# A gated mix of recurrent memory attention and a GLU, one core: one Wo piece kept in spare PSUM columns, one buffer for H

## The chip, the cores and the metric

The kernel runs on one core of a Trainium2 chip. The metric is the device time of one execution in microseconds (us); lower is better. Engines are named as in the profile: PE (matrix), PEld (its weight loads), DVE (vector), ACT (scalar), POOL, SP (it issues DMAs here). ACT issues DMAs too, on a queue of its own. SBUF is the working memory, PSUM the eight banks that PE writes.

## What is computed

x is 2048 rows of 640 (bf16). Two parts are mixed by a gate of each row. The costly part, `a`, runs over 64 segments of 32 rows, each with 8 memory rows that come from the segment before, so that the segments follow one another strictly:

```python
for s in range(n_seg):                                  # 64 segments, seg_len 32
    h = jnp.concatenate([mem, xs], axis=1)              # 8 memory rows + 32 rows of x
    q, k, v = (einsum('btd,dhe->bhte', h, W) for W in (Wq, Wk, Wv))   # 640 -> 32 heads x 192
    scores = einsum('bhqe,bhke->bhqk', q, k) * 192 ** -0.5            # causal, memory visible to all
    p = softmax(where(mask, scores, -1e9))
    o = einsum('bhqk,bhke->bhqe', p, v)
    o = einsum('bhte,hed->btd', o, Wo)
    mem = o[:, :8]                                      # goes on to the next segment
    outs.append(o[:, 8:])
b = (gelu(x @ w_gate) * (x @ w_up)) @ w_down
out = g * a + (1 - g) * b,   g = sigmoid((x * gate_w).sum(-1))
```

## The kernel before

**Stages.** The feed-forward part `b` comes first and goes to a scratch tensor in HBM. Then a left phase computes Q and K of the rows of x that become "left" columns of each segment (the last 8 of 32), for all segments at once, and stores them to scratch. Then the loop over 64 segments runs, about 27 us each by the profile.

**A segment** treats the 32 heads in four octets of eight. The list `PROG` gives the order in which a segment's work is recorded: for an octet `q` and `k` (`cmode`: 20 matmuls of 128x384 over five pieces of the weight, then an evacuation on ACT into a row buffer, `rows_sb`), `tq`, `tk` (`row_transp`: DVE transposes the rows into `Qs` and `Ks`), `v` (`v_oct`), `sc` (`scores`: a mask matmul, 16 score matmuls, then maximum and subtraction on DVE), `ex` (`softmax`: exponential on ACT, the rest on DVE), `pt` (`p_transp`), `pv` (`pv_oct`: PV matmuls, evacuated by one ACT copy and by two DVE copies, "uT lo" and "uT hi"), and `wo` (`wo_part`: 10 matmuls for each of 24 pieces of Wo, each piece a pair of 128-row chunks, accumulated in bank 7). In segments with s%4 == 0 `v_oct` also computes V of the left columns (20 more matmuls an octet), and the output of the four segments before goes out through five transposes and a store. At a segment's end ACT copies the new memory rows from bank 7 into H of the next segment (L1059, "mem evac"), and then its first matmul may start. Octets go through PSUM banks 0 to 4 in turn (`misc_bank`); the scores use 5 and 6. A bank is guarded as a whole: who writes it waits for all who read it.

**The order.** Each engine runs its instructions in the recorded order. A small recorder (`S_.add` with the regions read and written) derives the semaphore waits; a PE operation with several waits hands some of them to the last matmuls of the operation before. Nothing reorders at run time.

**The weights.** Wq, Wk, Wv and Wo together, 245760 B a partition, do not fit SBUF. A planner at build time makes pieces of 3072 B a partition (384 KB; Q, K, V) and 2560 B (320 KB; Wo), 84 of them; 61 stay in SBUF (`res_off`, loaded once by SP, some of them late, during segment 0) and 23 are streamed in every segment through a ring of five slots on SP's queue (`issue_ring`, L551; a slot is loaded again once PE has read it). The planner raises the number of streamed pieces until the rest fits `res_cap`, and spreads them evenly over a cost estimate of the segment (`COST`, `tcons`). The 23 are 14 of Q, K, V and 9 of Wo.

**Buffers that the change touches.** `Hb`, two buffers of 320 B a partition, holds H transposed (the five 128-row blocks of the segment's 32 columns); `x_load(s + 1)` fills the next one by a DMA on ACT's queue behind `k` of octet 2. `Ks` (1280 B a partition) is followed in memory by the two row buffers (`rows`, 1536 B). Two blocks of `Ks` stay zero from the start (memsets on POOL, L826 and L827). `left_fill(s, o)` (POOL, L834 and L838) copies the left columns of an octet from the staging buffer into `Qs` and `Ks`; that of octet 0 of the next segment is recorded behind the scores of octet 3, with `stg_load`, the DMA that fills the staging buffer. A Q, K or V group uses columns 0 to 383 of its bank (as 4-byte words), a PV group at most 320, so that the last 128 words of banks 0 to 4 are unused in the loop.

## Time and profile before

| | |
|---|---|
| median of 3 runs | 2105.77 us (2099.25 to 2106.26) |
| the profiled execution | 2103.78 us; span 2102.0 us |
| mean granted PE clock | 0.987 |
| busy over the span | PE 86%, PEld 55%, DVE 58%, ACT 29%, POOL 12% |
| moved by DMA | 622.11 MB, mean 296 GB/s; of it 576.63 MB on SP's queue |
| SP's weight loads | Wo 591, Wk 404, Wq 276, Wv 272; 4.8 to 5.3 us from issue to landing |

Each row of the profile's groups names a source line, an engine, an operation, its output and inputs (`arena` is all of SBUF, `ps` all of PSUM), shapes, and a count; then total busy time in us, the mean of one in ns, and the idle time of the engine ahead of them with what ended it. A row of a window begins with its start and end in us and its length. In a row of waits stand the total in us, how often, and the longest. "PE <- DMA" idle time is told both for the matmuls (PE) and for the weight loads that run ahead of them (PEld); the ends of matmuls are modelled, so a matmul that waits in mid-group can look busy.

### The profile page before, as it was taken

What the parts mean: (1) busy time and instruction counts of PE and PEld (TensorE: products, weight loads), DVE (VectorE), ACT (ScalarE), POOL (GpSimd) and SP (SyncE); (2) the same over time, 40 slices, a digit from 0 to 9 for tenths busy, and PEclk for the clock granted to TensorE, in tenths of its full rate; (3) what the DMA queues carried; (4) which work ended last, traced back from release to release, by engine and by line L of the source; (5) the groups of instructions that cost most, each with busy time, mean ns of one, the idle gap of its engine ahead of it and who ended that gap; (6) DMA issues with size and microseconds to landing.
All of it is one profiled execution on the core that took longest, in us unless ns stands there. A gap on an engine that the chain in (4) does not pass through costs nothing.

```text
span 2102.0 us, 92054 instructions
## 1 busy us (share of the span) xinstructions
PE 1797.9 (86%) x40486; PEld 1147.2 (55%) x40486; DVE 1223.0 (58%) x3928; ACT 619.4 (29%) x1468; POOL 241.8 (12%) x1060
## 2 busy tenths in 40 slices
PE   7899966888888888888889888888888888888887
PEld 3454433565555555555556555656555555555555
DVE  2222324666666666666666665666666666666666
ACT  2222212333333323332333332332323333323232
POOL 0000001111111111111111111111111111111111
PEclk9999998999999999999999999999999999999999
DMA  9412569999999999999999999999999999999998
GB/s 369 148 35 71 150 186 299 326 320 336 312 327 321 321 310 318 319 321 320 316 323 331 324 325 316 310 330 318 325 322 327 329 326 321 324 320 327 310 329 276
DMA packets 374252, 622.11 MB, mean 296 GB/s; under 512 B 81490, under 2 KB 250714, under 8 KB 373850
## 3 DMA queue, kind: packets, MB, share of 16 engines
q1 hardware_dynamic: 302842, 576.63, 80.9%
q10 hardware_dynamic: 71008, 39.60, 6.6%
q8 instruction: 316, 5.18, 1.0%
q14 instruction: 86, 0.70, 0.1%
HBM read 595.01 MB, written 21.10 MB: 293 GB/s over the span
## 4 chain that ended last, share of the span: by engine, by line
DMA 39%; PE 36%; DVE 16%; ACTq 3%; ACT 3%; issue 2%; SPq 0%; DVEq 0%
DMA arena<-in_A_Wk_dram 16%; DMA arena<-in_A_Wo_dram 9%; DMA arena<-in_A_Wv_dram 8%; PE ps L1017 8%; PE ps L868 8%; PE ps L895 5%; DMA arena<-in_A_Wq_dram 5%; PE ps L803 4%; DVE arena L971 3%; PE ps L732 2%; PE ps L729 2%; ACTq L818 2%; DVE arena L1004 2%; PE ps L988 2%; DVE arena L1002 2%
## 5 line engine op out<-in xcount | busy, mean ns | idle before, releaser
L868 PE MATMUL ps<-arena 128*32 128x384 bf16 x10240 | 547.3, 329 | 95.2 <-DMA arena<-in_A_Wk_dram 32.4
L1017 PE MATMUL ps<-arena 128*128 128x40 bf16 x15360 | 457.3, 180 | 58.7 <-DVE arena L1004 38.6
L1017 PEld LDWEIGHTS ps<-arena 128*128 128x128 bf16 x15360 | 425.5, 96 | 103.3 <-DVE arena L1004 50.0
L868 PEld LDWEIGHTS ps<-arena 128*32 128x32 bf16 x10240 | 246.6, 96 | 307.2 <-DMA arena<-in_A_Wk_dram 83.8
L872 ACT ACTIVATE arena<-ps 128x384 bf16<-128x384 f32 x512 | 251.4, 491 | 524.3 <-PE ps L868 450.6
L895 PE MATMUL ps<-arena 128*32 128x384 bf16 x6400 | 327.5, 331 | 54.0 <-DMA arena<-in_A_Wv_dram 31.5
L834 POOL COPY arena<-arena 128x96 bf16<-128x96 bf16 x256 | 67.5, 264 | 1611.3 <-PE ps L927 1063.2
L895 PEld LDWEIGHTS ps<-arena 128*32 128x32 bf16 x6400 | 150.9, 97 | 184.4 <-DMA arena<-in_A_Wv_dram 73.0
L878 DVE STREAM_TRANSPOSE arena<-arena 128x384 bf16<-128x384 bf16 x256 | 146.0, 570 | 90.4 <-ACT arena L872 90.4
L971 DVE TENSOR_TENSOR arena<-ps,arena 128x320 bf16<-128x320 bf16 x256 | 125.9, 492 | 88.9 <-PE ps L969 83.4
L988 PE MATMUL ps<-arena 128*128 128x160 bf16 (+1 forms) x768 | 131.2, 261 | 52.1 <-DVE arena L974 51.1
L906 ACT ACTIVATE arena<-ps 128x384 bf16<-128x384 f32 x256 | 125.8, 491 | 164.6 <-PE ps L895 164.3
L998 ACT ACTIVATE arena<-ps 128x320 bf16<-128x320 f32 x256 | 110.7, 432 | 215.4 <-PE ps L990 215.4
L955 DVE TENSOR_REDUCE arena<-ps 104x4 f32<-104x160 f32 x256 | 82.9, 324 | 153.4 <-ACT ps L953 151.4
L838 POOL COPY arena<-arena 64x32 bf16<-64x32 bf16 (+1 forms) x768 | 165.9, 216 | 47.4
L885 DVE STREAM_TRANSPOSE arena<-arena 64x128 bf16<-64x128 bf16 x512 | 145.4, 284 | 8.1
L953 ACT ACTIVATE ps<-ps 104x160 f32<-104x160 f32 x256 | 73.9, 289 | 202.6 <-DVE ps L943 185.5
L990 PE MATMUL ps<-arena 128*128 128x64 bf16 (+1 forms) x768 | 124.9, 203 | 0.0
L988 PEld LDWEIGHTS ps<-arena 128*128 128x128 bf16 x768 | 72.7, 98 | 93.0 <-DVE arena L974 71.0
L941 DVE TENSOR_REDUCE arena<-ps 104x4 f32<-104x160 f32 x256 | 81.2, 317 | 71.7 <-PE ps L927 71.7
L881 DVE STREAM_TRANSPOSE arena<-arena 128x256 bf16<-128x256 bf16 x256 | 111.5, 436 | 12.6 <-ACT arena L872 12.6
L1002 DVE CAST arena<-ps 64x160 bf16<-64x160 f32 x256 | 80.2, 313 | 46.4 <-PE ps L990 42.4
(71 smaller groups left out, 1672.1 us busy)
## 6 DMA issues: line engine op xcount, KB each, us to landing
arena<-in_A_Wo_dram SPq DMA_DIRECT2D x591, 320.0 KB, 4.8
arena<-in_A_Wk_dram SPq DMA_DIRECT2D x404, 384.0 KB, 5.2
arena<-in_A_Wq_dram SPq DMA_DIRECT2D x276, 384.0 KB, 5.1
arena<-in_A_Wv_dram SPq DMA_DIRECT2D x272, 384.0 KB, 5.3
left_qk_scratch<-arena ACTq DMA_DIRECT2D x16, 768.0 KB, 7.9
arena<-left_qk_scratch ACTq DMA_DIRECT2D x64, 192.0 KB, 4.5
arena<-in_A_x_dram SPq DMA_DIRECT2D x4, 640.0 KB, 15.6
xt_scratch<-arena ACTq DMA_DIRECT2D x4, 640.0 KB, 9.0
```

Source lines behind the costliest of these rows:

```text
L838: S_.add("pool", lambda e, a=a, b=b, lo=lo, hi=hi, sa=sa: e.tensor_copy(out=Ks[lo:hi, a:b, L:R], in_=stg[lo:hi, o, 1, sa:sa + b - a]), rea ...
L868: S_.add("pe", [lambda e, j=j, k=k, gv=gv: e.matmul(ps[32 * j:32 * j + 32, bank, 0:384].rearrange("p (c i) -> p c i", i=32), Hb[hb][:, k, ...
L872: S_.add("act", lambda e: e.activation(out=rows_sb[m], in_=ps[:, bank, 0:384], func=ACTF.Copy), reads=[r_ps[bank]], writes=[r_rows[m]], na ...
L878: S_.add("dve", lambda e: e.transpose(out=Qs[:, :, 0:L], in_=rows_sb[0].rearrange("p (c r) -> p c r", r=L)), reads=[r_rows[0]], writes=[r_ ...
L885: S_.add("dve", lambda e, a=a, lo=lo: e.transpose(out=Ks[lo:lo + 64, a:a + 4, 0:L], in_=src[lo:lo + 64, :, 1]), reads=[r_rows[1]], writes= ...
L895: return [lambda e, j=j: e.matmul(ps[32 * j:32 * j + 32, bk, 0:384], lhs, g_[:, 384 * j:384 * (j + 1)], start=(k == 0), stop=(k == KT - 1) ...
L906: S_.add("act", lambda e: e.activation(out=v_sb[o % NVB], in_=ps[:, bank, 0:384], func=ACTF.Copy), reads=[r_ps[bank]], writes=[r_v[o % NVB ...
L971: S_.add("dve", lambda e: e.tensor_tensor(out=PTm, in0=apx(pv[:, 512:616], [[64, 2], [0, 4], [1, R]]), in1=apx(mbd, [[0, 2], [1, 4], [0, R]]),
L988: return [lambda e: e.matmul(full, v[:, e0:e0 + 128], PTm[:, ia:ib], start=True, stop=False, skip_group_check=True), lambda e: e.matmul(pa ...
L990: lambda e: e.matmul(part, vl[:, e0:e0 + 128], PTl[:, ia:ib], start=False, stop=True, skip_group_check=True)]
L1002: S_.add("dve", lambda e: e.tensor_copy(out=u[0:64, :, 1, :], in_=ps[0:64, B, 0:W].rearrange("p (t r) -> p t r", r=R)), reads=[r_ps[B]], w ...
L1017: fns.append(lambda e, g_=g_, i=i, c=c, n=n, tl=tl, cc=cc, u=u: e.matmul(ps[:, OB, n * R:(n + 1) * R], g_[:, i, n * 128:(n + 1) * 128], u[ ...
```

## The change

One piece of Wo, (3, 19), the second pair of the last Wo group, is neither resident nor streamed. Before the loop `held_init` loads it from HBM, transposes it on PE, copies it back to SBUF, and transposes it again into the last 256 bf16 columns of banks 0 to 4, so that it stands there as it was: 5 x 256 columns are its 1280. In each segment `held_copy` (L591 of the changed kernel) copies it on ACT, one copy for each bank, into the memory of `Ks` and of the row buffers, which are idle by then; it is recorded after the first two pairs of Wo group 1 (`("pw", 0)`). After the last Wo group POOL zeroes the two blocks of `Ks` again (`k_zero`), and only then `left_fill` for the next segment follows. H has one buffer; `x_load` for the next segment moves behind `v` of octet 3, the last reader of H. The planner, with 320 B more and 2560 B less to place, streams 22 pieces: 13 of Q, K, V and 9 of Wo, at other places of the list; the left phase loads 8 pieces through the ring instead of 10. The three memory layouts' other parts stay.

```diff
-    wsA["H"] = al(2 * KT * L * 2)
+    wsA["H"] = al(KT * L * 2)
...
-    Hb = [bview(o_H + b * KT * L * 2, KT * L * 2).rearrange("p (k r) -> p k r", r=L) for b in range(2)]
+    Hb = [bview(o_H, KT * L * 2).rearrange("p (k r) -> p k r", r=L)] * 2
...
-            ("wo", 0), ("pt", 2), ("sc", 3), ("ex", 3), ("pv", 2), ("wo", 1), ("wo", 2, 0), ("pt", 3), ("wo", 2, 1),
+            ("wo", 0), ("pt", 2), ("sc", 3), ("ex", 3), ("pv", 2), ("wo", 1, 0), ("pw", 0), ("wo", 1, 1), ("wo", 1, 2), ("wo", 2, 0), ("pt", 3), ("wo", 2, 1),
             ("pv", 3), ("wo", 2, 2), ("wo", 3)]
...
+    HELD = (3, 19)
+    held_i = order.index(HELD)
...
-            best = min((i for i in range(npieces) if i not in streamed), key=lambda i: abs(tcons[i] - target))
+            best = min((i for i in range(npieces) if i not in streamed and i != held_i), key=lambda i: abs(tcons[i] - target))
             streamed.add(best)
-        if tot_bytes - sum(piece_size(order[i]) for i in streamed) <= res_cap:
+        if tot_bytes - GO - sum(piece_size(order[i]) for i in streamed) <= res_cap:
             break
...
+        if key == HELD:
+            return piece_view(key, o_held), r_held
...
+    o_held = wsB_off["K"]
+    r_held = sreg(o_held, GO)
+
+    def held_copy(seg):
+        flat = bview(o_held, GO)
+        for b in range(5):
+            S_.add("act", lambda e, b=b: e.activation(out=flat[:, 256 * b:256 * b + 256], in_=psb(b)[:, 768:1024],
+                                                      func=ACTF.Copy),
+                   reads=[r_ps[b]], writes=[r_held], name="held s%d %d" % (seg, b))
...
+    def held_init():
+        t1, r1 = bview(wsB_off["Q"], GO), sreg(wsB_off["Q"], GO)
+        t2, r2 = bview(wsB_off["vl"], GO), sreg(wsB_off["vl"], GO)
+        S_.add("sp", lambda e: e.dma_start(t1.rearrange("p (c n) -> p c n", n=Dm), piece_src(HELD)), writes=[r1],
+               dma_sem="held", name="held load")
+        for b, c0, nb in ((5, 0, 8), (6, 8, 2)):
+            S_.add("pe", [... e.transpose(psb(b)[:, ...], t1[:, 128 * c:128 * (c + 1)], ident) ...], ..., name="heldT")
+            S_.add("dve", lambda e, b=b, c0=c0, nb=nb: e.tensor_copy(out=t2[:, ...], in_=psb(b)[:, 0:128 * nb]), ...)
+        for b in range(5):
+            S_.add("pe", [... e.transpose(psb(b)[:, 768 + 128 * i:896 + 128 * i], t2[:, ...], ident) for i in range(2)], ..., name="heldTT")
+
     issue_ring(0, B_RING - 1)
+    held_init()
     S_.add("pool", lambda e: e.memset(pl_sb, 0.0), writes=[r_p])
-    S_.add("pool", lambda e: e.memset(Ks[64:128, 8:12, :], 0.0), writes=[r_Kz[0]])
-    S_.add("pool", lambda e: e.memset(Ks[0:64, 12:16, :], 0.0), writes=[r_Kz[1]])
+
+    def k_zero():
+        S_.add("pool", lambda e: e.memset(Ks[64:128, 8:12, :], 0.0), writes=[r_Kz[0]])
+        S_.add("pool", lambda e: e.memset(Ks[0:64, 12:16, :], 0.0), writes=[r_Kz[1]])
+
+    k_zero()
...
         elif s + 1 < NSEG:
             stg_load(s + 1)
-            left_fill(s + 1, 0)
...
                 if kind == "k" and i == 2:
-                    if s + 1 < NSEG:
-                        x_load(s + 1)
...
             elif kind == "v":
                 v_oct(s, i)
+                if i == NOCT - 1 and s + 1 < NSEG:
+                    x_load(s + 1)
+            elif kind == "pw":
+                held_copy(s)
...
                 wo_part(s, item)
+        if s + 1 < NSEG:
+            k_zero()
+            left_fill(s + 1, 0)
```

How this moves instructions, at three places of a segment. First SP's queue, from octet 1 to the segment's last ring load; each row is a load through the ring, and "x9" are nine in a row. Before:

```order
L551 DMA arena<-in_A_Wq_dram 128x1536
L551 DMA arena<-in_A_Wk_dram 128x1536
L551 DMA arena<-in_A_Wv_dram 128x1536
L551 DMA arena<-in_A_Wq_dram 128x1536
L551 DMA arena<-in_A_Wk_dram 128x1536 x2
L551 DMA arena<-in_A_Wv_dram 128x1536
L551 DMA arena<-in_A_Wq_dram 128x1536
L551 DMA arena<-in_A_Wk_dram 128x1536 x2
L551 DMA arena<-in_A_Wv_dram 128x1536
L551 DMA arena<-in_A_Wo_dram 128x2x640 x9
```

and now:

```order
L553 DMA arena<-in_A_Wq_dram 128x1536
L553 DMA arena<-in_A_Wk_dram 128x1536
L553 DMA arena<-in_A_Wv_dram 128x1536
L553 DMA arena<-in_A_Wq_dram 128x1536
L553 DMA arena<-in_A_Wk_dram 128x1536
L553 DMA arena<-in_A_Wv_dram 128x1536 x2
L553 DMA arena<-in_A_Wq_dram 128x1536
L553 DMA arena<-in_A_Wk_dram 128x1536
L553 DMA arena<-in_A_Wv_dram 128x1536
L553 DMA arena<-in_A_Wo_dram 128x2x640 x9
```

One load of Wk is gone in octet 2, V of octet 2 takes two where K took two, and octet 3 has one of Wk instead of two; octet 1's three stay. The nine loads of Wo stay nine.

Second ACT, from the DMA of x for the next segment (`xt_scratch`) to the copy of the memory rows that ends the segment (128x5x8); 128x384 are the evacuations of Q, K and V, 104x160 the exponential, 128x2x4x40 the evacuation of PV. Before:

```order
L631 DMA arena<-xt_scratch 128x160
L953 ACTIVATE ps<-ps 104x160
L998 ACTIVATE arena<-ps 128x2x4x40
L906 ACTIVATE arena<-ps 128x384
L872 ACTIVATE arena<-ps 128x384 x2
L953 ACTIVATE ps<-ps 104x160
L998 ACTIVATE arena<-ps 128x2x4x40
L906 ACTIVATE arena<-ps 128x384
L830 DMA arena<-left_qk_scratch 128x768
L953 ACTIVATE ps<-ps 104x160
L998 ACTIVATE arena<-ps 128x2x4x40 x2
L1059 ACTIVATE arena<-ps 128x5x8
```

and now, from what was the fifth of these rows (the evacuations of Q and K of octet 3):

```order
L910 ACTIVATE arena<-ps 128x384 x2
L990 ACTIVATE ps<-ps 104x160
L1035 ACTIVATE arena<-ps 128x2x4x40
L944 ACTIVATE arena<-ps 128x384
L646 DMA arena<-xt_scratch 128x160
L868 DMA arena<-left_qk_scratch 128x768
L990 ACTIVATE ps<-ps 104x160
L1035 ACTIVATE arena<-ps 128x2x4x40
L591 ACTIVATE arena<-ps 128x256 x5
L1035 ACTIVATE arena<-ps 128x2x4x40
L1101 ACTIVATE arena<-ps 128x5x8
```

The load of x stands now behind the evacuation of V of octet 3, ahead of the staging load, and the five copies of the held piece between the last two evacuations of PV.

Third PE, with the waits, from the transposes of P of octet 3 (128x104) through two pairs of Wo (L1017, now L1054) to its PV matmuls (L988 and L990, now L1025 and L1027); e_dve and e_act are the semaphores of DVE and ACT, d_ring1 one of the ring's. Before:

```order
L968 MATMUL ps<-arena 128x104
L969 MATMUL ps<-arena 128x104
L1017 MATMUL ps<-arena 128x40 x10
L1017 MATMUL ps<-arena 128x40 [waits d_ring1]
L1017 MATMUL ps<-arena 128x40 x9
L988 MATMUL ps<-arena 128x160 [waits e_dve]
L990 MATMUL ps<-arena 128x4x16
L988 MATMUL ps<-arena 128x160
L990 MATMUL ps<-arena 128x4x16
L988 MATMUL ps<-arena 128x320
L990 MATMUL ps<-arena 128x8x16
```

and now:

```order
L1005 MATMUL ps<-arena 128x104
L1006 MATMUL ps<-arena 128x104
L1054 MATMUL ps<-arena 128x40 x10
L1054 MATMUL ps<-arena 128x40 [waits d_ring4]
L1054 MATMUL ps<-arena 128x40 x8
L1054 MATMUL ps<-arena 128x40 [waits e_dve]
L1025 MATMUL ps<-arena 128x160 [waits e_act]
L1027 MATMUL ps<-arena 128x4x16
L1025 MATMUL ps<-arena 128x160
L1027 MATMUL ps<-arena 128x4x16
L1025 MATMUL ps<-arena 128x320 [waits e_act]
L1027 MATMUL ps<-arena 128x8x16
```

PV of octet 3 waits now for ACT at its start and once more in its second half: for the copies out of banks 3 and 4. The wait for DVE, which it had before, has gone to the Wo matmul ahead of it.

More of the change, by code (lines that the diff above doesn't have):

```diff
@@ L351, in _build @@
     o_H = wsA_off["H"]
-    Hb = [bview(o_H + b * KT * L * 2, KT * L * 2).rearrange("p (k r) -> p k r", r=L) for b in range(2)]
-    r_Hm = [sreg(o_H + b * KT * L * 2, 8) for b in range(2)]
-    r_Hxp = [sreg(o_H + b * KT * L * 2 + 8, KT * L * 2 - 8) for b in range(2)]
+    Hb = [bview(o_H, KT * L * 2).rearrange("p (k r) -> p k r", r=L)] * 2
+    r_Hm = [sreg(o_H, 8)] * 2
+    r_Hxp = [sreg(o_H + 8, KT * L * 2 - 8)] * 2
     o_Hx = wsA_off["Hx"]
@@ L506, in _build @@
             target = (k + 0.5) * tseg / nstream
-            best = min((i for i in range(npieces) if i not in streamed), key=lambda i: abs(tcons[i] - target))
+            best = min((i for i in range(npieces) if i not in streamed and i != held_i), key=lambda i: abs(tcons[i] - target))
             streamed.add(best)
-        if tot_bytes - sum(piece_size(order[i]) for i in streamed) <= res_cap:
+        if tot_bytes - GO - sum(piece_size(order[i]) for i in streamed) <= res_cap:
             break
         nstream += 1
-    resident_list = [i for i in range(npieces) if i not in streamed]
+    resident_list = [i for i in range(npieces) if i not in streamed and i != held_i]
     stream_list = [i for i in range(npieces) if i in streamed]
@@ L578, in load_late @@
             late_done[0] += 1
+    o_held = wsB_off["K"]
+    assert wsB_off["K"] + al(16 * R * 2) == wsB_off["rows"]
+    r_held = sreg(o_held, GO)
[5 more added lines that the diff above has]
+                   reads=[r_ps[b]], writes=[r_held], name="held s%d %d" % (seg, b))
     left_stream = [order[i] for i in stream_list if order[i][0] < 2]
```

14 lines of the change are left out of this document (12 added, 2 removed).

## The prediction

> **What bounds the kernel now.** I read the 40 slices and the queues of the page first, then the 62 whole segments as one window, then the waits inside them.
>
> ```profile
> DMA  9412569999999999999999999999999999999998
> GB/s 369 148 35 71 150 186 299 326 320 336 312 327 321 321 310 318 319 321 320 316 323 331 324 325 316 310 330 318 325 322 327 329 326 321 324 320 327 310 329 276
> ...
> q1 hardware_dynamic: 302842, 576.63, 80.9%
> ...
> DMA 39%; PE 36%; DVE 16%; ACTq 3%; ACT 3%; issue 2%; SPq 0%; DVEq 0%
> ```
>
> From the seventh slice on, which is the loop over segments, the 16 DMA engines are busy nine tenths or more in every slice at a flat 310 to 336 GB/s. Nearly all of it is queue q1, SP's weight stream. The last row is the chain that ended last: DMA has its largest share, with PE close behind.
>
> ```profile
> L1059 ACT ACTIVATE arena<-ps x63: 204/204/204, 361.5 to 2069.3; 128x40 bf16<-128x40 f32 x63
> ...
> 361.69:2069.55 1707.86, 1467.48 (x37483) 979.80 (x37483) 1104.52 (x3671) 525.65 (x1303) 226.10 (x992) 1.00 0.96 322
> ```
>
> L1059 ends each segment once, so 62 segments last 2069.3 - 361.5 = 1707.8 us, 27.55 us each. The window over them gives length, then busy time of PE, PEld, DVE, ACT and POOL, granted clock 1.00, DMA share 0.96, 322 GB/s. 27.55 us at 322 GB/s are 8.87 MB a segment. The 23 streamed pieces (14 of 384 KB, 9 of 320 KB) are 8.45 MB of that.
>
> Is the DMA the limit, or only busy? The waits in that window, for SP, PEld and PE:
>
> ```profile
> SPq L551 <- PE ps L868: 207.5, 226, 3.7
> ...
> PEld ps L868 <- DMA arena<-in_A_Wk_dram: 78.4, 155, 2.1
> PEld ps L895 <- DMA arena<-in_A_Wv_dram: 70.6, 117, 2.0
> PEld ps L868 <- DMA arena<-in_A_Wq_dram: 58.6, 124, 2.5
> PEld ps L1017 <- DMA arena<-in_A_Wo_dram: 21.8, 44, 1.7
> ...
> PE ps L895 <- DMA arena<-in_A_Wv_dram: 30.9, 44, 1.6
> PE ps L868 <- DMA arena<-in_A_Wk_dram: 28.8, 52, 1.7
> PE ps L868 <- DMA arena<-in_A_Wq_dram: 21.8, 31, 2.1
> PE ps L1017 <- DMA arena<-in_A_Wo_dram: 16.1, 32, 1.6
> ```
>
> SP issues the next piece as soon as PE frees a slot, and PE in turn waits for landings: 97.6 us by its matmuls, 229.4 us by its weight loads, 1.57 and 3.70 us a segment. So the pieces arrive just as they are needed, in both halves of a segment:
>
> ```profile
> 1509.10:1520.60 11.50, 9.48 (x300) 8.13 (x298) 7.02 (x25) 2.80 (x8) 0.92 (x4) 1.00 1.00 330
> 1520.60:1536.10 15.50, 13.57 (x287) 7.24 (x288) 10.10 (x34) 5.51 (x13) 2.74 (x12) 1.00 0.98 353
> ```
>
> The first is a Wo half, where a chain over DVE (softmax, transposes, evacuations) paces PE; the second the Q/K/V half of the next segment. The DMA rests in neither: it fills the ring while PE follows DVE.
>
> A natural experiment is in the trace. Every fourth segment (s%4 == 0) has 80 more V matmuls and five transposes. The sums over 15 segments with s%4 == 0, and over 15 with s%4 == 1:
>
> ```profile
> sum 427.11, PE 386.11 PEld 264.27 DVE 300.90 ACT 127.64 POOL 54.68; mean PE 25.74 PEld 17.62 DVE 20.06 ACT 8.51 POOL 3.65
> ...
> sum 402.21, PE 341.81 PEld 226.29 DVE 256.56 ACT 127.22 POOL 54.70; mean PE 22.79 PEld 15.09 DVE 17.10 ACT 8.48 POOL 3.65
> ```
>
> PE has 2.95 us more to do and the segment gets 1.66 us longer (28.47 against 26.81). It also stores output, 160 KB or 0.51 us at 322 GB/s:
>
> ```profile
> out_dram<-arena ACTq DMA_DIRECT2D x16, 160.0 KB, 5.4
> ```
>
> That leaves 1.15 us for 2.95 us of PE work, 0.39 us per us: PE's work is largely, not wholly, hidden.
>
> **The change part by part.**
>
> *One transfer fewer.* The planner's budget gains 320 B a partition from H and leaves out the held 2560 B. 22 pieces are then streamed, 13 of 384 KB and 9 of 320 KB: 393216 B less a segment. At 322 GB/s that is 1.22 us, the upper price, if time follows bytes alone. For the lower price I split the time: without DMA waits a segment is about 27.55 - 3.70 = 23.85 us of PE and chain; at 0.39 us per us these carry 9.3 us of the 27.55, so 18.25, or 66%, go with the transfers: 0.66 x 1.22 = 0.81 us. The middle is 1.02. I take 1.02 for three segments of four, and 0.81 where s%4 == 0, since PE is already 25.74 of 28.47 us busy there: 48 x 1.02 + 16 x 0.81 = 62 us. All 64 at the ends: 52 and 78 us.
>
> *Five copies on ACT.* PSUM to SBUF, 128x256 bf16:
>
> ```profile
> L712 ACT ACTIVATE arena<-ps 128x1024 bf16<-128x1024 bf16 x4 | 4.1, 1024 | 9.8 <-PE ps L698 9.8
> ...
> 1510.50 0.49 ACT L906 ACTIVATE arena<-ps 128x384 bf16<-128x384 f32 x1 [0.35 <-PE ps L895]
> ...
> 1513.79 0.28 ACT L953 ACTIVATE ps<-ps 104x160 f32<-104x160 f32 x1 [2.80 <-DVE ps L943]
> ...
> 1514.11 0.33 DVE L955 TENSOR_REDUCE arena<-ps 104x4 f32<-104x160 f32 x1 [0.35 <-ACT ps L953]
> 1514.47 0.18 DVE L957 RECIPROCAL arena<-arena 104x4 f32<-104x4 f32 x1
> ...
> 1515.32 0.33 DVE L1004 CAST arena<-ps 64x160 bf16<-64x160 f32 x1
> ...
> 1517.26 0.24 PE L988 MATMUL ps<-arena 128*128 128x160 bf16 x1 [0.29 <-DVE arena L974]
> ...
> 1517.72 0.44 ACT L998 ACTIVATE arena<-ps 128x320 bf16<-128x320 f32 x1 [3.30 <-PE ps L990]
> ...
> 1520.38 0.20 ACT L1059 ACTIVATE arena<-ps 128x40 bf16<-128x40 f32 x1 [2.22 <-PE ps L1017]
> ```
>
> 40 columns take 204 ns (L1059) and 1024 take 1024, 0.833 ns a column, so 256 take 384 ns and five 1.92 us. ACT is idle 3.30 us ahead of L998 at 1517.72, and the copies stand right there. Their cost is not length but the banks: the last of them wait for L1004 of octet 2 (its bank is read by DVE), which ends at 1515.65, and PV of octet 3 at 1517.26 then waits for the copies of banks 3 and 4. Two copies after L1004, each with some 0.05 us for its wait on the one before (an estimate: L957 starts 0.03 us after L955, on which it waits), end at 1516.52; the third, which only PV's second half needs, at 1516.95. PV starts at 1517.26 for DVE's sake. Cost nothing, with 0.3 us in hand even for the third; if a copy took 0.49 us, as 384 columns do, the third would end at 1517.27. PE's wait on ACT is then one already over.
>
> *H in one buffer.* The x load goes from ACT's place behind k 2 to behind the V evacuation (L906 above, 1510.99); what needs it is L1059 at 1520.38.
>
> ```profile
> arena<-xt_scratch ACTq DMA_DIRECT2D x64, 40.0 KB, 5.3
> ```
>
> It lands at about 1516.3, with 4 us in hand. Behind it on ACT stand the stage load and the exponential of octet 3, which waits for DVE until 1513.79. Leaving k 2 it frees ACT ahead of the exponential of octet 1: a gain of at most 0.3 us, taken as nothing.
>
> *POOL.* Two memsets are added, and four copies that filled the next segment's K and Q columns early now wait for the held piece's matmuls.
>
> ```profile
> L834 POOL COPY arena<-arena 128x96 bf16<-128x96 bf16 x256 | 67.5, 264 | 1611.3 <-PE ps L927 1063.2 <-DMA arena<-left_qk_scratch 361.7 <-PE ps L1017 186.3
> L838 POOL COPY arena<-arena 64x32 bf16<-64x32 bf16 x512 | 105.2, 206 | 31.5
> L838 POOL COPY arena<-arena 128x64 bf16<-128x64 bf16 x256 | 60.6, 237 | 15.8
> L826 POOL MEMSET arena<- 64x160 bf16 x1 | 0.2, 226 | 0.1
> ...
> 359.67 1.72 PE L1017 MATMUL ps<-arena 128*128 128x40 bf16 x62 [0.32 <-DVE arena L1004]
> ...
> 365.90 0.25 PE L916 MATMUL ps<-arena 128*40 128x160 bf16 x2
> ```
>
> 2 x 226 + 264 + 237 + 2 x 206 = 1365 ns, some 1.7 us with gaps, from the end of the held piece (22 of the 62 matmuls, at 360.3) to 362.0. The first scores, which need them, start at 365.90. Cost nothing; 3.9 us of cover.
>
> *Start.* A load of 320 KB, 20 transposes and two copies stand ahead of segment 0 on PE.
>
> ```profile
> arena<-in_A_x_dram SPq DMA_DIRECT2D x4, 640.0 KB, 15.6
> ...
> 137.28 1.29 PE L698 MATMUL ps<-arena 128*128 128x128 bf16 x20
> ...
> 322.32 3.23 PE L895 MATMUL ps<-arena 128*32 128x384 bf16 x37 [21.61 <-DMA arena<-left_xt_scratch]
> ```
>
> PE idles 21.61 us there for another queue's load. Even 15.6 us for the held load, 1.3 of transposes and three 1.02 us steps for the copies fit. Cost nothing, at worst a few us once; two ring loads fewer in the left phase are left at nothing too.
>
> Sum: 62 us. The profiled execution took 2103.78 us (span 2102.0), the median 2105.77; it lies 2 us below the median, and I take the gain off the median: 2044.
>
> **The rule that speaks against it.** The Trainium skill, Perfetto Trace Analysis, Identifying the Most-Contended Engine, calls occupancy of the DMA engines misleading and asks for HBM utilization; HBM Reference, Specifications, says that one core alone reaches about 425 GB/s. By that, 322 GB/s is 76%, the queue is not the limit, and the result is the third rival's. The trace is on its side in one row: 369 GB/s in the first slice.
>
> **The rivals.**
> 1. PE and the DVE chain take over early. Where a wait for a piece goes, one for DVE stands behind it. If only the matmuls' idle time, 1.57 of the 3.70 us, is really lost to the DMA, 0.42 x 1.22 = 0.52 us a segment come back: 33 us, 2073. For it: L988 at 1517.26 waits for DVE, not for a piece. Against: the flat 322 GB/s.
> 2. The full 1.22 us and somewhat more, as a shorter queue also lands each piece sooner: 80 us, 2026.
> 3. The rate is not the limit; each piece's turn-around is. PE then loses one of 23 waits: 97.6/23 to 229.4/23, 4 to 10 us: 2096 to 2102, within the 0.5% (10.5 us) that a measurement of this kernel can tell. Against: the DMA rests in neither half.
> 4. Slower: the copies hold PV of octet 3. Three copies must fit from 1515.65 to the second half of PV, which is some 0.2 us behind 1517.26: 1.8 us. To lose the 62 us and 10.5 more, PV must be 1.13 us late in each segment, so a copy must take 0.98 us with its wait. At the 1.02 us of L712, with 0.05 of wait, it is 3.2 - 1.8 = 1.4 us, 90 us lost, 2134. For it: all five are chained by waits on ACT itself. Against: the two rows on ACT give 384 ns.
>
> **How the numbers follow.** Forecast 0.62, first rival 0.22, second 0.04, third 0.07, fourth 0.05. Faster: 0.62 + 0.22 + 0.04 = 0.88; same 0.07; slower 0.05. The forecast alone spans 52 to 78 us, 2028 to 2054. The range reaches from just under that, 2025, into the first rival's 2073: 2025 to 2075. About 0.15 stays out.
>
> **What would show it.** Right: a segment of 26.5 us, DMA share still 0.94 to 0.96, PE's weight-load waits for DMA down by about a quarter, five copies near 384 ns that end before PV of octet 3. Wrong: a DMA share well under 0.94 with the segment hardly shorter (rivals 1, 3); PE's L1025 waiting for ACT's L591 (rival 4); L1101 waiting for the x load, or L954 for POOL.

## The result and the profile after

The changed kernel takes 2046.27 us (median of 4 runs, 2043.35 to 2054.95); the kernel before, on the same chip, 2102.51 us (4 runs, 2098.40 to 2106.26). The ratio is 0.974, its 95% interval 0.9702 to 0.9777. The profiled execution took 2043.35 us, with a span of 2041.5 us: 60.5 us less than the span of before. The forecast was 2044.

The page of the changed kernel: DMA share and rate of the 40 slices, SP's queue, and the engines' shares of the chain that ended last.

```profile
DMA  9412659999999999999999999999999999999998
GB/s 372 157 39 65 151 156 298 325 315 329 318 321 310 307 317 317 315 311 322 311 328 319 322 313 322 312 317 317 326 312 319 311 326 316 327 324 312 315 317 277
...
q1 hardware_dynamic: 293482, 551.07, 79.6%
...
PE 27%; DVE 25%; DMA 22%; ACT 4%; issue 3%; ACTq 0%; SPq 0%; DVEq 0%
```

SP's queue moved 25.56 MB less (551.07 for 576.63). The rate did not rise; it fell a little. In the chain DMA went from 39% to 22%.

The end of a segment (L1101, formerly L1059), and the window over the 62 whole segments, with columns as before:

```profile
L1101 ACT ACTIVATE arena<-ps x63: 204/204/204, 357.4 to 2010.8; 128x40 bf16<-128x40 f32 x63
...
357.56:2011.02 1653.46, 1448.16 (x37483) 986.20 (x37483) 1104.24 (x3671) 638.38 (x1612) 255.21 (x1118) 1.00 0.95 318
```

A segment lasts 1653.46 / 62 = 26.67 us, 0.88 us less than the 27.55 of before; 62 of them give 54.4 us. The first of these rows starts 4.1 us earlier than it did (357.4 against 361.5), and the rest of the 60.5 us, some 2 us, is at the end. The waits for weights in that window:

```profile
PEld ps L906 <- DMA arena<-in_A_Wq_dram: 66.4, 141, 2.1
PEld ps L933 <- DMA arena<-in_A_Wv_dram: 48.9, 91, 1.7
PEld ps L906 <- DMA arena<-in_A_Wk_dram: 21.2, 39, 1.8
PE ps L933 <- DMA arena<-in_A_Wv_dram: 21.1, 29, 1.3
PE ps L906 <- DMA arena<-in_A_Wq_dram: 20.8, 32, 1.7
PEld ps L1054 <- DMA arena<-in_A_Wo_dram: 16.6, 38, 1.4
PE ps L906 <- DMA arena<-in_A_Wk_dram: 9.5, 15, 1.4
PE ps L1054 <- DMA arena<-in_A_Wo_dram: 6.2, 12, 1.0
```

The weight loads wait 153.1 us (229.4 before), the matmuls 57.6 us (97.6 before): 0.93 us a segment for 1.57. Of the 0.88 us that a segment gained, 0.65 us stands in the matmuls' rows and 0.31 us in PE's busy time (1448.16 us for 1467.48), in which a wait in mid-group is counted; the matmuls' waits for DVE grew a little, from 109 to 113 us.

What the change added, in the timeline of one segment and of the start (in brackets the idle time ahead of a row and what ended it):

```profile
299.63 1.25 PE L846 MATMUL ps<-arena 128*128 128x128 bf16 x10 [5.19 <-DMA arena<-in_A_Wo_dram]
...
318.89 3.07 PE L933 MATMUL ps<-arena 128*32 128x384 bf16 x36 [12.22 <-DMA arena<-left_xt_scratch]
...
1498.40 0.80 ACT L591 ACTIVATE arena<-ps 128x256 bf16<-128x256 bf16 x2
...
1499.77 1.22 ACT L591 ACTIVATE arena<-ps 128x256 bf16<-128x256 bf16 x3 [0.57 <-DVE arena L1041]
...
1501.41 0.23 PE L1025 MATMUL ps<-arena 128*128 128x160 bf16 x1
...
1503.48 0.23 POOL L862 MEMSET arena<- 64x160 bf16 x1 [10.49 <-PE ps L1054]
1504.45 0.77 POOL L876 COPY arena<-arena 128x64 bf16<-128x64 bf16 x3
...
1509.88 0.25 PE L954 MATMUL ps<-arena 128*40 128x160 bf16 x2
```

The five copies split into two and three around DVE's evacuation of octet 2, as worked out; the last ends at 1500.99, 0.42 us before PV of octet 3. POOL is done 4.7 us before the scores need it, and L1101, which writes into H, never waits for the load of x: all its waits are for PE. At the start the held load made PE wait 5.19 us, which came out of the wait for the other queue's load: that shrank from 21.61 to 12.22 us, and V starts at 318.89 (322.32 before). Over the whole run the copies held up nobody; the row "who waited for it" is empty:

```profile
L591 ACT ACTIVATE arena<-ps x320: 384/384/389, 351.2 to 2033.4; 128x256 bf16<-128x256 bf16 x160
...
who waited for it (us, times):
```

So the time comes from the stream. The question for the experiments is by which law: bytes at a fixed rate, as the forecast had it, or something else that gives nearly the same number.

### The profile page after: what moved, and what is told of

Same layout as the page of the kernel before. It is cut to its first block, busy times and chain, and to the rows that moved or that the text cites. A ratio compares the mean times of both kernels' runs of the same rounds, so it can differ in the third digit from the quotient of the medians.

```text
span 2041.5 us, 92471 instructions
## 1 busy us (share of the span) xinstructions
PE 1782.8 (87%) x40498; PEld 1156.4 (57%) x40506; DVE 1223.5 (60%) x3930; ACT 735.8 (36%) x1788; POOL 271.2 (13%) x1186
## 3 DMA queue, kind: packets, MB, share of 16 engines
q1 hardware_dynamic: 293482, 551.07, 79.6%
q8 instruction: 316, 5.18, 1.0%
## 4 chain that ended last, share of the span: by engine, by line
PE 27%; DVE 25%; DMA 22%; ACT 4%; issue 3%; ACTq 0%; SPq 0%; DVEq 0%
PE ps L906 11%; DMA arena<-in_A_Wv_dram 7%; DMA arena<-in_A_Wq_dram 7%; PE ps L1054 7%; PE ps L933 4%; DMA arena<-in_A_Wo_dram 4%; DMA arena<-in_A_Wk_dram 4%; DVE arena L1008 4%; DVE arena L1041 3%; DVE arena L992 3%; DVE arena L923 3%; DVE arena L1039 2%; DVE arena L996 2%; ACT arena L910 2%; DVE arena L919 2%
## 5 line engine op out<-in xcount | busy, mean ns | idle before, releaser
L1054 PE MATMUL ps<-arena 128*128 128x40 bf16 x15360 | 455.7, 179 | 67.5 <-DVE arena L1041 44.4
L1054 PEld LDWEIGHTS ps<-arena 128*128 128x128 bf16 x15360 | 423.3, 96 | 113.1 <-DVE arena L1041 56.6
L906 PEld LDWEIGHTS ps<-arena 128*32 128x32 bf16 x10240 | 255.6, 96 | 263.8 <-DMA arena<-in_A_Wq_dram 72.6
L933 PEld LDWEIGHTS ps<-arena 128*32 128x32 bf16 x6400 | 158.2, 97 | 158.7 <-DMA arena<-in_A_Wv_dram 51.1
L1025 PE MATMUL ps<-arena 128*128 128x160 bf16 (+1 forms) x768 | 129.6, 258 | 43.8 <-DVE arena L1011 42.7
L990 ACT ACTIVATE ps<-ps 104x160 f32<-104x160 f32 x256 | 74.2, 290 | 190.4 <-DVE ps L980 183.2
L591 ACT ACTIVATE arena<-ps 128x256 bf16<-128x256 bf16 x320 | 123.1, 385 | 48.3 <-DVE arena L1041 40.6
L1027 PE MATMUL ps<-arena 128*128 128x64 bf16 (+1 forms) x768 | 124.1, 202 | 0.7 <-DMA arena<-in_A_Wv_dram 0.6
L1025 PEld LDWEIGHTS ps<-arena 128*128 128x128 bf16 x768 | 72.7, 97 | 88.6 <-DVE arena L1011 62.7
L862 POOL MEMSET arena<- 64x160 bf16 x64 | 14.5, 227 | 788.5 <-PE ps L1054 678.1
```

The source lines that it names most:

```text
L906: S_.add("pe", [lambda e, j=j, k=k, gv=gv: e.matmul(ps[32 * j:32 * j + 32, bank, 0:384].rearrange("p (c i) -> p c i", i=32), Hb[hb][:, k, ...
L933: return [lambda e, j=j: e.matmul(ps[32 * j:32 * j + 32, bk, 0:384], lhs, g_[:, 384 * j:384 * (j + 1)], start=(k == 0), stop=(k == KT - 1) ...
L1025: return [lambda e: e.matmul(full, v[:, e0:e0 + 128], PTm[:, ia:ib], start=True, stop=False, skip_group_check=True), lambda e: e.matmul(pa ...
L1027: lambda e: e.matmul(part, vl[:, e0:e0 + 128], PTl[:, ia:ib], start=False, stop=True, skip_group_check=True)]
L1054: fns.append(lambda e, g_=g_, i=i, c=c, n=n, tl=tl, cc=cc, u=u: e.matmul(ps[:, OB, n * R:(n + 1) * R], g_[:, i, n * 128:(n + 1) * 128], u[ ...
```

## The experiments

Ratios are to the kernel before on the same chip, each with its 95% interval; the kernel before took 2100.49, 2099.15 and 2099.52 us in the three sets of runs. The first four runs weigh the forecast's law, bytes at a fixed rate (theory A in the expectations), against its rivals and against the change's other parts; the later ones weigh it against the slots of the ring, their number, their turns and the places of the pieces. In the expectations of the first four, rival B says that the full bytes come back and that the copies, the zeroing and the late fill give some of it away again; rival C says that the moved load of x is the source. Theory D is set out in the expectation of "The turn too".

**Is it the removed transfer at all?** The changed kernel, made to stream 23 pieces again:

```diff
-        if tot_bytes - GO - sum(piece_size(order[i]) for i in streamed) <= res_cap:
+        if tot_bytes - GO - sum(piece_size(order[i]) for i in streamed) <= res_cap and nstream >= 23:
```

> The changed kernel with the stream of the kernel before: 23 pieces, the same ones, so that one resident piece fewer is kept and the room stays empty. Held piece, copies, zeroing, late fill, one buffer for H, all stay. Theory A: the change without its transfer is worth nothing: 2098 to 2106, the kernel before within 0.2%. Rival B: 0.3 us a segment slower, 2115 to 2125. Rival C: 10 to 20 us faster, 2083 to 2093.

Measured: 2097.72 us, 0.9992 (0.9971 to 1.0013), as theory A had it. Everything else that the change does, held piece, copies, one buffer for H, moved load of x, is together worth nothing that these runs can tell (6 us faster to 3 us slower). The gain comes with the 23rd transfer: with its removal, and with the new places that the planner then gives the other 22.

**The copies alone.** The changed kernel without its five copies in each segment:

```diff
-                held_copy(s)
+                pass
```

> The changed kernel without the five copies of a segment; zeroing, late fill and the rest stay (the held piece's matmuls read what lies in the buffers, so that part of Wo is not applied rightly). Theory A: the copies cost nothing; their profile shows them over 0.26 us or more ahead of PV: 2043 to 2050, the same as the changed kernel. Rival B: 20 us faster than it, 2022 to 2030.

2047.47 us, 0.9737 (0.9708 to 0.9766), against 2046.27 and 0.974 with them. They are free.

**The moved load of x alone**, in the kernel before:

```diff
-                    if s + 1 < NSEG:
-                        x_load(s + 1)
...
+                if i == NOCT - 1 and s + 1 < NSEG:
+                    x_load(s + 1)
```

> The kernel before with the load of x behind v of octet 3, still two buffers: that move alone. Theory A: within 0.3% of before, 2096 to 2106; what it gives is in segments with s%4 == 3, where three DMAs stood on ACT ahead of the exponential of octet 1 and PE waited 0.71 us for DVE's L960 behind it: 0.3 us in 16 segments, 5 us. Rival C: 10 to 20 us faster, 2083 to 2093.

2098.22 us, 0.9979 (0.9958 to 1.0): 2 us, at most 9. It is not the source either.

**Bytes without a slot.** In the kernel before, one K piece, the first of the two that octet 2 streams, loads 128 of its 1536 columns: 11/12 of its bytes are gone, but it still takes its slot and its turn in the ring.

```diff
-            S_.add("sp", lambda e, slot=slot, key=key: e.dma_start(piece_view(key, ring_off[slot]), piece_src(key)),
+            dst, src = piece_view(key, ring_off[slot]), piece_src(key)
+            if key == (1, 2, 0):
+                dst, src = (dst[:, 0:1, 0:128], src[:, 0:1, 0:128]) if key[0] == 3 else (dst[:, 0:128], src[:, 0:128])
+            S_.add("sp", lambda e, dst=dst, src=src: e.dma_start(dst, src),
```

> The kernel before; of one streamed piece, (1, 2, 0) of Wk, the loop loads only 128 of 1536 columns, so that the transfer all but goes and nothing else changes (the rest of the piece's slot holds old data: that part of K is not computed from its weights). 0.36 MB of 8.78 MB a segment go. Theory A (the gain is one transfer's time on a DMA that PE follows closely, 66% to 100% of its bytes' share, and the rest of the change costs nothing): 0.75 to 1.12 us a segment, 48 to 72 us off, 2030 to 2055, as far as the whole change went (2046). Rival B (the full bytes come back, 1.12 us, and the change's copies, zeroing and late fill give 0.3 us a segment back): 72 us off, 2031, clearly faster than the whole change. Rival C (part of the gain is the load of x that left ACT's place behind k 2, not the transfer): 35 to 45 us off, 2058 to 2068.

2092.77 us, 0.9964 (0.9943 to 0.9985). This is 8 us (3 to 12), 0.12 us a segment, where bytes at 322 GB/s would give 1.1 us a segment. All three expectations missed. The profile of this kernel caught the longest of its 12 executions (2081.79 to 2100.74 us), so its length says nothing; but its DMA shows what happened. Over 59 segments, the stretch from 6 to 7 us behind a segment's start has a mean DMA share of 0.83 and 239 GB/s, where the kernel before has 0.98 and 351 GB/s. The DMA engines idled for part of the hole instead of fetching ahead: the next load may go out only when PE gives back the next slot in order, and the shortened piece keeps its slot until PE has read it, as a whole one does. It did not even land much sooner, 4.3 us from issue to landing where the whole pieces of Wk in the same run took 4.9; when all ring loads are short (the floor run below), they land in 1.8 to 2.1 us:

```profile
arena<-in_A_Wk_dram SPq DMA_DIRECT2D x340, 384.0 KB, 4.9
...
arena<-in_A_Wk_dram SPq DMA_DIRECT2D x64, 32.0 KB, 4.3
```

**The turn too.** The same piece is taken out of the stream altogether (it reads the memory of a resident piece); the other 22 keep their old, uneven places.

```diff
+    GONE = (1, 2, 0)
+    stream_list = [i for i in stream_list if order[i] != GONE]
...
+        if key == GONE:
+            return piece_view(key, res_off[(1, 2, 1)]), r_res[(1, 2, 1)]
...
     def left_piece(key):
+        if key == GONE:
+            return piece_view(key, res_off[(1, 2, 1)]), r_res[(1, 2, 1)]
```

> The kernel before with piece (1, 2, 0) of Wk taken out of the stream altogether: 22 loads and 22 turns of the ring a segment, the other 22 where they were; its matmuls read a resident piece in its place (that part of K is computed from other weights). Short loads had given 0.36% where bytes alone would have given 2.3 to 3.4%. Theory D (slots: a piece costs a turn of the ring, issue to landing to use, 27.55 x 5 / 23 = 6.0 us for each slot, and the DMA moves faster the more is in flight; a short piece holds its slot as long as a whole one): 22 turns, 0.85 to 1.2 us a segment off, 2023 to 2046. Rival P (plan: the gain of the change came from its new, even spread of the streamed pieces, and a piece less is worth the 8 us of the short load): 2085 to 2095.

2071.11 us, 0.9859 (0.9829 to 0.989): 28 us, half of the gain. It lies between the two expectations (2023 to 2046 and 2085 to 2095), so that each of them held a part of the cause.

```profile
359.32:2038.29 1678.97, 1459.76 (x37483) 984.44 (x37483) 1103.66 (x3671) 525.66 (x1303) 225.38 (x992) 0.99 0.94 313
```

27.08 us a segment. The hole is there as well, later, where the next loads would have been released: at 11 to 13 us of a segment the mean over 59 is 0.89 and 0.85 (289 and 274 GB/s), where before it was 0.97 and 0.94 (334 and 328).

**The spacing too.** The changed kernel's 22 evenly spread pieces and its places of H and x, but no held piece: no load, copies, or zeroing; its Wo piece reads a resident one's memory.

```diff
-            return piece_view(key, o_held), r_held
+            return piece_view(key, res_off[(3, 18)]), r_res[(3, 18)]
...
-    held_init()
...
+            left_fill(s + 1, 0)
...
-                held_copy(s)
+                pass
...
-        if s + 1 < NSEG:
-            k_zero()
-            left_fill(s + 1, 0)
```

> The changed kernel without the held piece's work: no loading and transposing at the start, no copies, no zeroing, and the fill of the next segment's columns back behind the scores; its planner's 22 pieces in their even places stay, one H buffer and the later load of x too. The held piece's matmuls read a resident piece in its place (that part of Wo is not applied). With it the 22 pieces stand in the new places, where e5_drop (2071) has a hole in the old ones. If the even spread is the other half of the gain and the held piece costs nothing: 2040 to 2050, as the changed kernel. If the spread is worth nothing: 2065 to 2075, and the changed kernel's work would have to gain by itself.

2044.24 us, 0.9747 (0.972 to 0.9773), the same as with the held piece (0.974).

```profile
354.70:2012.77 1658.07, 1450.66 (x37483) 987.73 (x37483) 1104.31 (x3671) 525.00 (x1302) 225.38 (x992) 1.00 0.95 317
```

From 1678.97 to 1658.07 us for the 62 segments, 20.9 us by the new places of the 22 pieces (with the moved load of x, some 2 us by its own run), and 4.6 us ahead of the first of them, which hold the left phase, with 8 ring loads instead of 9, and segment 0. So the removed piece's gain has three steps: its bytes 8 us, its turn 20 more, the even spread of what is left, with the shorter stretch ahead of the loop's whole segments, 27 more.

**One piece more.** The kernel before with 24 streamed pieces:

```diff
-        if tot_bytes - sum(piece_size(order[i]) for i in streamed) <= res_cap:
+        if tot_bytes - sum(piece_size(order[i]) for i in streamed) <= res_cap and nstream >= 24:
```

> The kernel before with 24 pieces streamed, 15 of 384 KB: one transfer and one turn more, spread anew by the planner, nothing else. Theory D: one turn of 6.0 / 5 = 1.2 us more a segment, less what PE's own work covers: 0.85 to 1.2 us, 2155 to 2177. Theory A: 0.81 to 1.22 us, 2152 to 2178. Rival P: within 0.5% of before.

2159.58 us, 1.0282 (1.025 to 1.0315), within what was expected; its 62 segments:

```profile
358.14:2126.63 1768.49, 1499.48 (x37483) 985.44 (x37483) 1104.64 (x3671) 524.79 (x1302) 225.38 (x992) 0.99 0.96 325
```

28.52 us a segment: 22, 23 and 24 pieces take 26.67, 27.55 and 28.52 us. With five slots a slot is loaded again every 6.06, 5.99 and 5.94 us (segment x 5 / pieces): nearly constant. Of such a turn of 6 us, 4.8 to 5.3 us are the flight of the load, from issue to landing, so that a slot is loaded again about 1 us after its piece has landed. "So many bytes at 322 GB/s" and "so many turns of 6 us in five slots" tell the same tale in these three; the next run parts them.

**A sixth slot.** The changed kernel with a ring of six; the slot's space costs one resident piece, so that 23 pieces are streamed, 14 of Q, K, V and 9 of Wo as before the change: the old bytes.

```diff
-    B_RING = int(opts.get("ring", 5))
+    B_RING = int(opts.get("ring", 6))
```

> The changed kernel with six slots in the ring instead of five; the planner pays for the slot with one more streamed piece, 23, the very ones of the kernel before. Same bytes a segment as before, 8.78 MB. Theory D: 23 turns over 6 slots; more in flight moves 333 GB/s or more, 26.2 us a segment, 86 us off before: about 2014, faster than the changed kernel by 1 to 2%. Theory A (bytes at the DMA's rate of 322 GB/s): 2095 to 2103, as before.

2025.09 us (4 runs, 2023.04 to 2030.28), 0.9648 (0.9618 to 0.9679): 21 us faster than the changed kernel, and the fastest of all that were run. By bytes at a fixed rate it had to fall back to 2095 to 2103: that theory is refuted. (The changed kernel with the very same 23 pieces in five slots is the first experiment: 2097.72 us.)

```profile
359.97:1998.33 1638.36, 1445.16 (x37483) 985.76 (x37483) 1104.00 (x3671) 637.92 (x1612) 253.37 (x1116) 1.00 0.98 336
```

With the same 23 pieces a segment takes 26.43 us instead of 27.55. The DMA, at a share of 0.96, had 4% more to give after all (336 GB/s for 322), and the weight loads' waits for weights fell to 100.1 us from 229.4:

```profile
PEld ps L906 <- DMA arena<-in_A_Wk_dram: 41.9, 82, 1.7
PEld ps L933 <- DMA arena<-in_A_Wv_dram: 28.4, 60, 2.0
PEld ps L906 <- DMA arena<-in_A_Wq_dram: 26.9, 76, 1.5
PEld ps L1054 <- DMA arena<-in_A_Wo_dram: 2.9, 6, 1.1
```

**The floor.** The changed kernel, all ring loads cut to 128 columns: what remains when the stream costs next to nothing. The streamed weights are then mostly old data.

```diff
-            S_.add("sp", lambda e, slot=slot, key=key: e.dma_start(piece_view(key, ring_off[slot]), piece_src(key)),
+            dst, src = piece_view(key, ring_off[slot]), piece_src(key)
+            if True:
+                dst, src = (dst[:, 0:1, 0:128], src[:, 0:1, 0:128]) if key[0] == 3 else (dst[:, 0:128], src[:, 0:128])
+            S_.add("sp", lambda e, dst=dst, src=src: e.dma_start(dst, src),
```

> The changed kernel; all ring loads of the loop bring 128 columns of one row block only (0.7 MB a segment instead of 8.1), the rest of the slots being old data, so that the transfers all but go and PE and its chain remain. By the weight loads' waits for DMA (2.47 us a segment in the changed kernel's profile) a segment takes 24.2 us without them: 2046 less 64 x 2.47, 1888. By the matmuls' own waits (0.93 us) it takes 25.7: 1985.

1975.51 us, 0.9408 (0.9376 to 0.944), near the 1985 that the matmuls' waits gave and far from the 1888 by the weight loads' waits.

```profile
349.75:1944.43 1594.68, 1426.53 (x37483) 999.09 (x37483) 1103.97 (x3671) 636.85 (x1613) 253.35 (x1116) 1.00 0.19 44
```

25.72 us a segment, paced by PE and by its waits for DVE (140 us in all). The matmuls' waits had told this: 26.67 - 0.93 = 25.74 for the changed kernel. That it agrees so closely is partly luck: without the stream PE's busy time fell by 22 us and its waits for DVE rose by 27. The weight loads' waits (2.47 us) would have said 24.20; they run ahead, and a wait of theirs is often over before the matmul needs it.

**Seven and eight slots**, at 24 and 25 streamed pieces:

```diff
-    B_RING = int(opts.get("ring", 5))
+    B_RING = int(opts.get("ring", 7))
```

(and 8 for 7).

> The changed kernel with seven slots and, to pay for them, 24 streamed pieces: 0.39 MB a segment more than six slots and 23 pieces (2025). Theory D: more in flight moves more, but the DMA's busy share was 0.98 with six slots, so little is left to gain: 9.17 MB at 340 GB/s are 27.0 us, against 26.4 us with six: 2040 to 2065. If slots alone count (24/7 is less than 23/6): 2000 to 2015.

> Eight slots, 25 streamed pieces. Theory D: the DMA's own rate is the limit now, 9.5 MB at 340 GB/s: 28.1 us, 2100 to 2130, worse than with seven. If slots alone count: 1990 to 2010.

Seven: 2026.13 us, 0.9644 (0.9626 to 0.9662), no better than six, and between the two expectations. Eight: 2079.76 us, 0.9911 (0.9887 to 0.9934), worse as the first expectation said, though by less; slots alone would have made it the fastest. Their windows, seven first:

```profile
354.37:1995.73 1641.36, 1456.02 (x37483) 1008.18 (x37483) 1104.35 (x3671) 637.72 (x1613) 253.26 (x1117) 0.99 1.00 350
```

```profile
354.95:2045.74 1690.79, 1471.86 (x37483) 1012.83 (x37483) 1105.20 (x3671) 637.29 (x1613) 253.38 (x1116) 0.97 1.02 366
```

The rate goes on rising, 350 and 366 GB/s at shares of 1.00 and 1.02, and a piece lands later; the loads of Wo with five (the kernel before), six, seven and eight slots, from issue to landing in the last column:

```profile
arena<-in_A_Wo_dram SPq DMA_DIRECT2D x591, 320.0 KB, 4.8
```

```profile
arena<-in_A_Wo_dram SPq DMA_DIRECT2D x591, 320.0 KB, 5.0
```

```profile
arena<-in_A_Wo_dram SPq DMA_DIRECT2D x591, 320.0 KB, 5.9
```

```profile
arena<-in_A_Wo_dram SPq DMA_DIRECT2D x654, 320.0 KB, 6.5
```

So a turn gets longer with the slots, 6.9, 7.7 and 8.7 us with six, seven and eight: the 6 us belong to five slots. Eight slots all but end the matmuls' waits for weights (3.4 us in the largest row left), so that 366 GB/s is what PE then asks for, and yet the segment is 27.27 us. The Wo matmuls of that kernel, busy time and then their idle time by cause:

```profile
L1054 PE MATMUL ps<-arena 128*128 128x40 bf16 x14880 | 456.9, 181 | 96.7 <-issue 45.9 <-DVE arena L1041 36.4 <-DVE arena L1011 10.1
```

45.9 us of "issue", a wait for nothing that the profile shows; with six slots that entry is 6.7 us. Over all matmuls it is 71 us for 11, and PE's busy time is 27 us longer (1471.86 for 1445.16) at a granted clock of 0.97 for 1.00; the waits for weights and for DVE, 36 us shorter, do not make up for it. What the "issue" time is was not found. That the fuller DMA delays something that PE needs besides weights, such as its instructions (the page lists a DMA queue named "instruction", 5.18 MB), is a guess that no run tested.

**The copies doubled**, each of the five twice:

```diff
                 held_copy(s)
+                held_copy(s)
```

> The changed kernel with the five copies of a segment made twice, one set behind the other. The copies of the first set that wait for DVE's last evacuation of octet 2 (banks 2, 3, 4) and the whole second set then follow it: 8 x 0.41 = 3.3 us from 1515.65 in the terms of the first profile, where PV of octet 3 needs the last two banks by 1517.3 to 1517.5. PV is 1.4 to 1.6 us late; the floor kernel says that 1.1 us of a segment are still slack to the DMA, of which a part is in that half: 0.7 to 1.5 us a segment, 2090 to 2140. If ACT's copies were hidden by the DMA anyway: 2046.

2175.19 us, 1.0353 (1.0335 to 1.0371): 129 us above the changed kernel, and above all that was expected (2090 to 2140).

```profile
1475.69 3.29 ACT L591 ACTIVATE arena<-ps 128x256 bf16<-128x256 bf16 x8 [0.65 <-DVE arena L1041]
...
1478.62 0.21 PE L1054 MATMUL ps<-arena 128*128 128x40 bf16 x1 [1.75 <-ACT arena L591]
```

PE now waits 1.75 us for the copies. The forecast's fourth rival had the right mechanism and the wrong size of copy: five copies of 384 ns leave 0.4 us, ten do not fit. The rest of the loss goes with a lower clock (last section).

## Why the prediction was right, and where its steps were not

*The time.* Forecast 2044, measured 2046.27; the gain forecast at 62 us was 56.2 by the medians (2102.51 - 2046.27), inside the 52 to 78 given for the forecast alone. The time came closer than the gain because the kernel before ran 3.3 us faster this time (2102.51 for 2105.77), which is luck.

*One transfer fewer: right number, wrong law.* The failed step is "At 322 GB/s that is 1.22 us, the upper price, if time follows bytes alone". Time does not follow bytes: taking 11/12 of a piece's bytes gave 0.12 us a segment, and the old bytes with a sixth slot gave back 1.12 us (27.55 to 26.43). What is limited is how often five slots can turn: one turn lasts 6.0 us, so that a piece would cost 6.0 / 5 = 1.2 us of segment if the turns were all; it costs 0.88 (22 to 23) or 0.97 (23 to 24) as measured. That the number came out is luck: the price by bytes is the piece's share of the bytes of a segment, 1.22 us, and the price by turns is a 23rd of the segment, 1.20 us, and with 23 pieces of nearly one size these can hardly differ. The rate of 322 GB/s is itself made by the five slots.

*"the DMA rests in neither half".* It was taken from a share of 0.98 to 1.00 and served against the third rival. But a share of that size is not a rate at its end: it was 0.96 at 322 GB/s, 0.98 at 336, 1.00 at 350 and 1.02 at 366, and what exceeds 1 cannot be a part of the time. The rule of the Trainium skill that the prediction weighed (Perfetto Trace Analysis, Identifying the Most-Contended Engine: occupancy misleads for the DMA) was right, and the rows agree. The third rival, "each piece's turn-around", was thus the true mechanism with the wrong price: 4 to 10 us for one of 23 waits, where the turn and the new spacing are worth 56.

*The split of the time.* "Without DMA waits a segment is about 27.55 - 3.70 = 23.85 us" took the weight loads' waits. Measured: 25.72. The matmuls' waits, 1.57, which the first rival held for the real ones, give 25.98. So the first rival's premise was right too, but its price (0.52 us) was not, since the removal took 0.88 out of 27.55 - 25.72 = 1.83 us that there were to gain. This slip hardly moved the forecast: with 25.72 for 23.85 the lower price would have been 64% of 1.22, 0.78 us for 0.81. The mean over all segments was forecast at 0.97 and came to 0.88.

*"1.02 for three segments of four, and 0.81 where s%4 == 0"* did not show. Sums over 15 segments of the changed kernel with s%4 == 0 and over 15 with s%4 == 1:

```profile
sum 414.32, PE 381.56 PEld 264.35 DVE 300.00 ACT 155.56 POOL 61.77; mean PE 25.44 PEld 17.62 DVE 20.00 ACT 10.37 POOL 4.12
...
sum 391.74, PE 337.93 PEld 230.46 DVE 256.73 ACT 154.02 POOL 61.54; mean PE 22.53 PEld 15.36 DVE 17.12 ACT 10.27 POOL 4.10
```

27.62 and 26.12 us: 0.85 less in the first kind, 0.70 in the second (28.47 and 26.81 before). Yet the thought behind it, that the stream is worth less where PE has more to do, is borne out by the floor run. The same sums there:

```profile
sum 409.21, PE 377.83 PEld 264.73 DVE 299.68 ACT 155.46 POOL 61.57; mean PE 25.19 PEld 17.65 DVE 19.98 ACT 10.36 POOL 4.10
...
sum 374.60, PE 333.73 PEld 234.60 DVE 256.77 ACT 153.75 POOL 60.90; mean PE 22.25 PEld 15.64 DVE 17.12 ACT 10.25 POOL 4.06
```

27.28 and 24.97 us: there were 1.19 us to gain where s%4 == 0 and 1.84 where s%4 == 1. The removal took more of the smaller sum; why is not shown. The largest gain, 1.22 us, is in s%4 == 3 (28.03 to 26.82 by its 14 segments), and most of that is not the removed piece: in the changed kernel with 23 pieces these segments already take 27.07 us, and in the kernel before with the moved load of x alone 27.62 (one profile each).

*Copies, H, POOL, start: right.* Five copies of 384 ns, no wait for them, 0.4 us in hand where 0.3 was worked out; the load of x lands in time; POOL has 4.7 us in hand where 3.9 was worked out; the held load hides in a wait that was there.

*"Two ring loads fewer in the left phase are left at nothing":* the first end of a segment came 4.1 us earlier, but this is segment 0 too, and how much of it those two loads are worth is not shown. The kernel before with 24 pieces, which has all ten, reaches it at 357.9 us, and two runs with eight, the copies left out and the copies doubled, at 356.6 and 358.7. Of the things that would show it, the segment (26.5 forecast, 26.67) and the DMA share (0.95) came as said; the weight loads' waits fell by a third instead of a quarter.

## What to carry to other kernels

A DMA queue that is busy 96% of the time behind a ring of few buffers may be limited by the ring: give it one more slot, even at the price of one more transfer, before bytes are counted (here 23 pieces in six slots beat 22 in five by 21 us, while 25 pieces in eight slots were 33 us slower than 22 in five). When a transfer is taken out of a ring that is refilled in order, spread the remaining ones anew, since up to half of the gain lay in that. For what a stream costs, read the matmuls' waits rather than those of the weight loads that run ahead, and test with the transfers cut short.

## What the runs showed of the hardware

The rate of the loads is no constant: 322, 336, 350 and 366 GB/s with five to eight slots, while the share of the DMA engines went only from 0.96 to 1.02 and the landing of a 320 KB piece from 4.8 to 6.5 us (five slots: the kernel before).

A short wait of PE can cost twice. In the kernel with doubled copies, three windows around the wait of 1.75 us, with PE's busy time first and the granted clock third from the end:

```profile
1473.20:1476.90 3.70, 3.25 (x107) 3.00 (x107) 2.36 (x10) 2.43 (x7) 0.00 (x0) 1.00 0.95 317
1476.90:1478.60 1.70, 0.00 (x0) 0.00 (x0) 0.23 (x2) 1.54 (x6) 0.00 (x0) 0.91 0.84 269
1478.60:1482.40 3.80, 3.63 (x87) 3.23 (x87) 0.65 (x2) 0.82 (x3) 0.94 (x4) 0.59 0.70 183
```

Behind the wait the clock stands at 0.59 for 3.8 us. The window over the 62 segments of that kernel, and the matmuls' waits for the copies in it:

```profile
358.86:2139.66 1780.80, 1530.29 (x37483) 1043.55 (x37483) 1104.40 (x3671) 756.07 (x1922) 253.20 (x1116) 0.92 0.91 295
```

```profile
PE ps L1025 <- ACT arena L591: 54.2, 46, 1.5
...
PE ps L1054 <- ACT arena L591: 23.3, 16, 1.7
```

The waits themselves are 77.5 us, 1.25 a segment; but the 62 segments are 127 us longer than the changed kernel's, and PE's busy time for the same matmuls is 82 us longer (1530.29 for 1448.16) at a mean clock of 0.92. The two sum to more than 127, because the matmuls' other waits shrink meanwhile, those for weights from 58 to 36 us and those for DVE from 113 to 102. The Trainium skill, TensorE: Matmul & The Clock Gate, HAM oscillation, warns of idle gaps of PE above some 3.4 us; here the clock fell after one of 1.75 us, which followed a stretch in which PE was busy 88% of the time. The length of a wait alone does not decide it. In the kernel before, PE once waited 1.74 us for a piece of Wk, and the clock stayed at 1.00:

```profile
1300.18:1303.88 3.70, 3.70 (x90) 1.83 (x82) 1.88 (x6) 1.97 (x4) 0.31 (x2) 1.00 0.95 295
1303.88:1305.62 1.74, 0.00 (x2) 0.01 (x2) 0.77 (x2) 0.00 (x0) 0.60 (x3) 1.00 0.89 265
1305.62:1309.42 3.80, 3.53 (x76) 1.78 (x77) 2.15 (x9) 1.67 (x4) 0.00 (x0) 1.00 1.02 382
```

What sets the two apart no run here shows.
